# Output weights of a linear-attention block in four products by head group, re-blocked through DRAM, and phi(K) in one vector step

## The chip, the cores and the metric

The kernel runs on one core of one Trainium2 chip. The core has a matrix engine (TensorE, PE), a vector engine (DVE), a scalar engine (ACT), a general engine (GpSimd, POOL) and a queue engine (SyncE, SP) that issues most of the DMAs. Weight loads of TensorE are listed apart as PEld. Each engine works through its own queue in order and waits on semaphores. The metric is the device time of one execution in microseconds (us); the time before is 190.59 us, the median of three runs (190.52 to 190.61).

## The reference

The input x has 2048 tokens of 448 numbers, in bf16. The first half is a linear-attention block with 16 heads of 28, the second half a gated feed-forward block of width 1792. Cut to what matters:

```python
def phi(t): return where(t > 0, t + 1, exp(t)) + 1e-6
q, k, v = heads(layernorm(x) @ wqkv)
kv  = einsum("bhsd,bhse->bhde", phi(k), v)      # per head, summed over all tokens
z   = einsum("bhsd->bhd", phi(k))
num = einsum("bhqd,bhde->bhqe", phi(q), kv)
den = einsum("bhqd,bhd->bhq", phi(q), z) + 1e-6
h   = x + (num / den) @ wo
y   = layernorm(h)
out = h + (gelu(y @ w_gate) * (y @ w_up)) @ w_down
```

## The kernel before

**Tiles.** The tokens are sixteen tiles of 128 rows (t = 0 to 15), and from the query stage on eight pairs of tiles (p = 0 to 7). Channels of the attention come as four groups of four heads, 112 channels each.

**Stage 1, layer norm and projections.** Each tile of x is normalised (statistics at lines 413 and 414), transposed (tiles 0 to 3 on TensorE at line 443, the others by DMA at line 455) and projected to K and Q (line 469). The normalised tile xnn is padded with a column block of ones, so it is 512 wide. For K, ACT takes the exponential (`ek`, line 480), DVE clamps it (`ck`, line 481) and DVE forms phi(K) = max(k, eps) + clamped exponential (`pk`, line 482). Four products per tile (line 488) add xnn-transposed times phi(K) into four PSUM banks over all tiles. The ones give z in the last bank. Most Q projections are held back, as filler for the next stage.

**Stage 2, kv and the output weights.** The four banks are evicted (lines 514 to 521: `z1`, `z0`, `evpD_3`, `evpA_0`, `evpA_1`, `evpD_2`). Sixteen small products with the value weights (line 527, `kv`) give kv for each head. DVE masks it into `kvz` (line 531, `kvm`), laid out with zeros between the groups and a copied piece (`kvd`, line 536). Seven products (line 547) multiply it by wo, so that the result `w2` stands in four row blocks of 128, 128, 128 and 64 channels; the first three blocks get contributions from two head groups each, hence seven. Two DMAs (`dws0`, `dws1`) copy the halves of three blocks crosswise into `w2s`, so that each 64-row block exists in both halves of the partitions.

**Stage 3, query pairs.** For a pair p, DVE and POOL make phi(Q) and the denominators (`cqP`, `aqP`, `t1p`, `drP`, `rdP`, lines 582 to 589) and the normalised query (`pnP`, line 590). It is transposed, for pair 0 on TensorE (line 599) and for the others by a DMA that SP issues (`oT_p`, line 605). The attention output is the transposed query times `w2`. Pair 0 uses eight full products (line 617, `out1_0` and `out1_1`). Pairs 1 to 7 use fourteen products of 64 rows in two passes (lines 627 and 628, `outA_p` and `outB_p`): two such products run at the same time in the two row halves of TensorE, one for each tile of the pair. The second pass waits for the first to end, since it swaps the halves.

**Stage 4, feed-forward.** DVE adds the residual (`hr_t`, line 633), takes statistics, and the normalised tile is transposed (`hT_t`, line 665). Gate and up are computed in chunks: `gu2_v` for two tiles (chunks 0 to 13) and `gu4_v` for four (14 to 55), lines 731 and 733, 64-row products in both halves. ACT applies gelu (line 751, `ge`), DVE multiplies (line 753, `hm`). Even chunks use PSUM banks 0 and 6, odd ones 1 and 7, so a chunk starts only when both `hm` of the chunk two before it are done. The down products are `downA_p`, `downB_p` (line 697) and line 678 at the end.

**What sets the order.** Every piece of work is a task with a number, in the sequence in which the code creates it. `ORDERS` lists, engine by engine, the numbers in the order of that engine's queue; the waits follow from which task reads or writes which buffer. `HOLD` says, for tasks with several waits, which one is put first. The order around the change on TensorE is: `q_5 q_4 kv q_7 q_8 w2_2 w2_0 w2_1 q_9 w2_3 tro_1 tro_0 q_6 out1_1 out1_0 q_10 ... q_14 q_15 trh_1 trh_0 outA_1 outB_1 gu2_0 gu2_1 outA_2 gu2_2 gu2_3 outB_2`. On SP it is: `dwg0 dwu0 dwg1 dwu1 dws0 dws1 oT_1 oT_2 dwd oT_3`, where `dwg`, `dwu` and `dwd` load the gate, up and down weights.

Of the kernel before, what the change touches and what calls it, by code (L numbers as in the profile page):

```python
# [822 lines left out]
```

## Time and profile before

| what | value |
|---|---|
| median of three runs | 190.59 us |
| span of the profiled execution, first to last instruction | 188.3 us |
| TensorE busy | 184.3 us, 98% |
| DVE busy | 129.3 us, 69% |
| ACT busy | 76.5 us, 41% |
| POOL busy | 50.0 us, 27% |
| granted TensorE clock | 1.000 |

The span leaves out what lies around the first and last instruction, 2.3 us against the median. Busy time of TensorE includes the time in which a product drains through the engine, which overlaps the next product. The pace of a stage is therefore read from the distance between the starts of two instructions. In the rows of the timeline the columns are start, length, engine, line, operation, output and inputs, shape and count; in brackets stands the idle time before and what ended it. In the rows of groups the columns after the count are busy us, mean ns of one, and the idle time before.

### The profile page before, as it was taken

Reading aid. Unit: us, or ns where it says so; the run is one execution under the profiler, and the core shown is the slowest. Engines: PE = TensorE matmul, PEld = TensorE weight load, DVE = VectorE, ACT = ScalarE, POOL = GpSimd, SP = SyncE. Lnnn points to the kernel's source line nnn. Section 1 sums busy time; section 2 is a strip of 40 time slices with the busy share of each in tenths; the row PEclk is TensorE's granted clock in tenths of the full one; section 3 lists DMA queues with packets and bytes.
Section 4 is the critical chain, followed back from the end, with each engine's and each line's share of the span. In section 5 each row is a group of like instructions: output and inputs, shape, how many; then the busy total and the mean of one; then the engine's idle time right before and its main releaser. Section 6 shows DMA issues by size and latency. Waiting matters only on the chain.

```text
span 188.3 us, 4459 instructions
## 1 busy us (share of the span) xinstructions
PE 184.3 (98%) x1813; PEld 109.2 (58%) x1813; DVE 129.3 (69%) x330; ACT 76.5 (41%) x220; POOL 50.0 (27%) x91
## 2 busy tenths in 40 slices
PE   7999999999999999999999999999999999999994
PEld 7545555555688788965554555555545545454554
DVE  4999959999899998786796762562645244335432
ACT  3878752799963231432234222321242222224100
POOL 6067910704505686033614000206100000000000
PEclk9999999999999999999999999999999999999999
DMA  5996458999393526820005720000096000002024
GB/s 169 387 231 88 96 104 194 218 222 174 65 320 64 95 52 116 84 52 0 0 3 98 144 54 0 0 3 2 3 135 111 3 0 24 3 0 98 3 79 140
DMA packets 35076, 17.11 MB, mean 91 GB/s; under 512 B 26864, under 2 KB 33648, under 8 KB 35056
## 3 DMA queue, kind: packets, MB, share of 16 engines
q1 hardware_dynamic: 34432, 16.32, 41.1%
q10 hardware_dynamic: 624, 0.52, 0.8%
q8 instruction: 14, 0.23, 0.5%
q14 instruction: 6, 0.05, 0.1%
HBM read 8.26 MB, written 1.84 MB: 54 GB/s over the span
## 4 chain that ended last, share of the span: by engine, by line
PE 94%; DVE 3%; DMA 1%; issue 0%
PE ps L733 38%; PE ps L697 19%; PE ps L469 12%; PE ps L731 9%; PE ps L488 6%; PE ps L627 3%; PE ps L678 3%; PE ps L628 2%; DMA x_sb<-in_A_x_dram 1%; DVE st L413 1%; PE ps L617 1%; PE ps L547 1%; PE ps L527 1%; PE ps L443 0%; PE ps L654 0%; DVE den L572 0%
## 5 line engine op out<-in xcount | busy, mean ns | idle before, releaser
L733 PE MATMUL ps<-hnT,wgu_sb 64*128 64x512 bf16 (+1 forms) x490 | 88.8, 333 | 0.0
L731 PE MATMUL ps<-hnT,wgu_sb 64*128 64x512 bf16 (+1 forms) x490 | 88.6, 333 | 0.0
L751 ACT ACTIVATE gl<-ps 128x256 bf16<-128x256 f32 x112 | 36.6, 383 | 85.3 <-PE ps L731 84.4
L753 DVE TENSOR_TENSOR hh<-ps,gl 128x256 bf16<-128x256 f32 x112 | 42.1, 416 | 41.4 <-ACT gl L751 41.3
L733 PEld LDWEIGHTS ps<-hnT,wgu_sb 64*128 64x128 bf16 x490 | 45.2, 94 | 32.9 <-DVE hh L753 3.4
L731 PEld LDWEIGHTS ps<-hnT,wgu_sb 64*128 64x128 bf16 x490 | 45.4, 94 | 2.5
L697 PE MATMUL ps<-wd_sb,hh 64*128 64x448 bf16 x392 | 41.5, 349 | 0.0
L697 PEld LDWEIGHTS ps<-wd_sb,hh 64*128 64x128 bf16 x392 | 23.2, 94 | 14.5
L469 PE MATMUL ps<-wqk_sb,xnT 128*128 128x448 bf16 x128 | 27.4, 353 | 0.0
L413 DVE BATCH_NORM_STATS2 st<-x_sb 128x6 f32<-128x448 bf16 x32 | 19.2, 612 | 1.8 <-DMA x_sb<-in_A_x_dram 1.7
L585 POOL TENSOR_TENSOR t<-pq,zbc 128x448 f32<-128x448 bf16 x12 | 12.3, 1042 | 23.7 <-DVE pq L583 22.0
L469 PEld LDWEIGHTS ps<-wqk_sb,xnT 128*128 128x128 bf16 x128 | 11.9, 98 | 11.4 <-DVE pk L482 0.8
L488 PE MATMUL ps<-pk,xnn 128*128 128x448 bf16 x64 | 13.9, 352 | 0.0
L627 PE MATMUL ps<-w,pqnT 64*128 64x448 bf16 x49 | 11.5, 349 | 0.1
L425 POOL TENSOR_SCALAR ln<-mv 128x2 f32<-128x2 f32 x7 | 2.0, 291 | 35.2 <-DVE mv L414 35.0
L480 ACT ACTIVATE e<-ps 128x448 bf16<-128x448 f32 x16 | 8.5, 539 | 5.6 <-PE ps L469 5.5
L628 PE MATMUL ps<-pt_sb,pqnT 64*128 64x448 bf16 x42 | 10.2, 350 | 0.0
L633 DVE TENSOR_TENSOR x_sb<-ps,x_sb 128x448 bf16<-128x448 f32 x16 | 9.6, 616 | 0.7 <-PE ps L628 0.6
L662 POOL TENSOR_SCALAR hn<-x_sb,nm,rs 128x448 bf16<-128x448 bf16 x14 | 9.9, 719 | 0.4
L482 DVE SCALAR_TENSOR_TENSOR pk<-ps,e 128x448 bf16<-128x448 f32 x16 | 9.8, 617 | 0.1
L488 PEld LDWEIGHTS ps<-pk,xnn 128*128 128x128 bf16 x64 | 6.3, 98 | 5.9 <-DVE pk L482 0.3
L453 POOL TENSOR_SCALAR xnn<-x_sb,nm,rs 128x448 bf16<-128x448 bf16 x12 | 8.9, 744 | 2.2 <-ACT rs L422 1.9
(85 smaller groups left out, 160.5 us busy)
## 6 DMA issues: line engine op xcount, KB each, us to landing
out_dram<-x_sb SPq DMA_DIRECT2D x15, 112.0 KB, 1.8
wd_sb<-in_B_w_down_dram SPq DMA_DIRECT2D x1, 1568.0 KB, 8.4
x_sb<-in_A_x_dram SPq DMA_DIRECT2D x3, 448.0 KB, 5.9
wgu_sb<-in_B_w_gate_dram SPq DMA_DIRECT2D x1, 896.0 KB, 12.1
wgu_sb<-in_B_w_up_dram SPq DMA_DIRECT2D x1, 896.0 KB, 16.5
wgu_sb<-in_B_w_gate_dram SPq DMA_DIRECT2D x1, 672.0 KB, 6.1
wgu_sb<-in_B_w_up_dram SPq DMA_DIRECT2D x1, 672.0 KB, 8.5
wo_sb<-in_A_wo_dram SPq DMA_DIRECT2D x1, 392.0 KB, 7.5
```

The lines of the kernel that those rows point to most:

```text
L413: op("dve", lambda e: e.bn_stats(st[:, t, :], src_ap), [b_src], [b_st[t]], "bnst%s_%d" % (tag, t))
L469: ins = e.matmul(ps[:, bk, 0:D], xnT[:, t, k, :], wqk_sb[:, k, c0:c0 + D], start=(k == 0), stop=(k == 3))
L488: ins = e.matmul(ps[:, BK_PT[c], 0:D], xnn[:, t % XN_R, c * 128:(c + 1) * 128], pk[:, ip, :], start=(t == 0), stop=(t == T - 1))
L585: op("pool", lambda e, n=n: e.tensor_tensor(t1[:, n, :], pq[:, a + n, :], zbc[:, :], ALU.mult), [b_pq[a + n]] + b_z, [b_t1[n]], "t1p_%d" % ...
L627: e.matmul(ps[:, BK_OUT[0], 0:D], pqnT[ra, i2, sg // 2, :], w2[ra, sg // 2, :], start=(sg == 0), stop=(sg == 5))
L628: ins = e.matmul(ps[:, BK_OUT[1], 0:D], pqnT[rb, i2, 3 + (sg + 1) // 2, :], (w2 if sg == 6 else w2s)[rb, sg // 2, :], start=(sg == 0), sto ...
L662: op("pool", lambda e, t=t, sh=sh: e.tensor_scalar(hn[:, sh, 0:D], x_sb[:, t, :], nm2[:, t:t + 1], rs2[:, t:t + 1], ALU.add, ALU.mult), [b ...
L697: ins = e.matmul(ps[:, bko[half][n], 0:D], hh[rows, j, sl[n]], wd_sb[rows, j, :], start=(j == 0 and (half == 0 or p == 6)), stop=(j == NJ ...
L731: first = e.matmul(psG[:, jj * N:(jj + 1) * N], wgu_sb[A_, k, j * 128:(j + 1) * 128], hnT[A_, ka_, c0:c0 + N], start=(k == 0), stop=(k == ...
L733: ins = e.matmul(psU[:, jj * N:(jj + 1) * N], wgu_sb[B_, k, j * 128:(j + 1) * 128], hnT[B_, kb_, c0:c0 + N], start=(k == 0), stop=(k == NK ...
L751: G.add("act", lambda e, gi=gi, cs_=cs_, psG=psG: e.activation(gl[:, gi, cs_], psG[:, cs_], AF.Gelu_apprx_tanh), r=[b_ps[BK_G[i]]], w=[b_g ...
L753: op("dve", lambda e, dst=dst, srcU=srcU, srcL=srcL: e.tensor_tensor(dst, srcU, srcL, ALU.mult), [b_ps[BK_U[i]], b_glh], [b_ar[j_][t % HR] ...
```

## The change

The change has five parts.

1. *phi(K) in one step.* A row of ones is written into the padding of the K weights (`w1row`), where the normalised tile has ones, so the projection gives k + 1. ACT takes exp(k + 1 - 1) with a bias of -1. One DVE operation forms max(min(e, 1), k + 1). The clamp `ck` is gone. The 1e-6 of phi is added later: `pk` gets an extra column of 1e-6 (`pkeps`), the sums get a 449th column, and the evictions add it (`ecol` copies two such columns for ACT; z gets 2048 x 1e-6).
2. *Output weights by head group.* `kvz` holds the masked kv densely; four products of 112 rows each give `w2g`, one block for each head group. `kvd`, the zero padding of `kvz` and the two crosswise copies are gone.
3. *Pairs 0 and 1 use `w2g` as it is*, with eight products for a pair. Their normalised queries are written with each group padded to 128 columns, so the transposition of pair 1 has 1024 columns, not 896.
4. *Pairs 2 to 7 keep their 64-row products.* The blocks come through DRAM: one DMA writes `w2g` to a DRAM buffer (`dw2w`), two DMAs read it back as seven blocks of 64 rows into each half of the partitions (`dw2r0`, `dw2r1`). The buffer `w2p` lies over the sums and the value weights, which are dead by then.
5. *New orders and holds.* All five queues are ordered anew, and `HOLD` names one wait for most tasks. On TensorE the order around the change is now: `q_5 q_9 kv q_4 q_7 w2_1 w2_0 w2_2 q_8 w2_3 tro_0 tro_1 q_6 out1_0 out1_1 q_10 ... q_14 q_15 trh_0 trh_1 out1_2 out1_3 gu2_0 gu2_1 gu2_2 gu2_3 outA_2 gu2_4 outB_2 gu2_5 gu2_6 outA_3 downA_0 outB_3 gu2_7`. On SP: `dwg0 dwu0 dwg1 dwu1 oT_1 dw2w dw2r0 dw2r1 oT_2 dwd oT_3`. On DVE, after the output of pair 1: `hr_2 hr_3 bnst2_2 bnst2_3 drP_3 hm1_0 hm0_0 bnag2_3 bnag2_2 rdP_3 cqP_5 hm1_1 hm0_1 cqP_7 pnP_3 hm0_2 hm1_2 aqP_5 hm1_3 cqP_4 cqP_6 hm0_3 wrap_2 wrap_3 aqP_4 hr_5 hm0_4 hm1_4`. On ACT, `evhA_0` now comes before `eq_15`. On POOL, one memset of `pqn` and `mhalf` now come before `ones`, which the warm-up products read.

```diff
+        pv_sb = sb("pv_sb", [128, 8, D], BF16)
+        pt_sb, wv_sb, w2p = pv_sb[:, 0:4, :], pv_sb[:, 4:8, :], pv_sb[:, 0:NK, :]
...
-        pk = sb("pk", [128, PK_R, D], BF16)
+        pk = sb("pk", [128, PK_R, D + 2], BF16)
...
-        w2 = sb("w2", [128, 4, D], BF16)
+        w2g = sb("w2g", [GW, NG, D], BF16)
+        w2d = nc.dram_tensor("w2_bounce", [D, D], BF16)
...
+        op("dve", lambda e: e.memset(wqk_sb[64:65, 3, D:2 * D], 1.0), [b_wpad[0]], [b_w1r], "w1row")
...
-        op("pool", lambda e: e.memset(kvz[:, GW:15 * GW], 0.0), [], [b_kvm], "kvzpad")
+        for i_ in range(2):
+            op("pool", lambda e, i_=i_: e.memset(pqn[:, i_, :].rearrange("p (n g c) -> p n g c", n=2, g=NG)[:, :, :, GW:128], 0.0), [], b_pqn[i_], "pqnpad_%d" % i_)
...
-            eks.append(act_exp(lambda e: e.activation(e1[:, i, :], psK, AF.Exp), [b_ps[bk]], [b_e1[i]], "ek_%d" % t))
-            op("dve", lambda e: e.tensor_scalar(e1[:, i, :], e1[:, i, :], 1.0 + EPS, 0.0, ALU.min, ALU.max), [b_e1[i]], [b_e1[i]], "ck_%d" % t)
-            op("dve", lambda e: e.scalar_tensor_tensor(pk[:, ip, :], psK, EPS, e1[:, i, :], ALU.max, ALU.add), [b_ps[bk], b_e1[i]], [b_pk[ip]], "pk_%d" % t)
+            eks.append(act_exp(lambda e: e.activation(e1[:, i, :], psK, AF.Exp, bias=neg1[:, 0:1]), [b_ps[bk], b_neg1], [b_e1[i]], "ek_%d" % t))
+            op("dve", lambda e: e.scalar_tensor_tensor(pk[:, ip, 0:D], e1[:, i, :], 1.0, psK, ALU.min, ALU.max), [b_ps[bk], b_e1[i]], [b_pk[ip]], "pk_%d" % t)
...
-                        ins = e.matmul(ps[:, BK_PT[c], 0:D], xnn[:, t % XN_R, c * 128:(c + 1) * 128], pk[:, ip, :], start=(t == 0), stop=(t == T - 1))
+                        ins = e.matmul(ps[:, BK_PT[c], 0:D + 1], xnn[:, t % XN_R, c * 128:(c + 1) * 128], pk[:, ip, 0:D + 1], start=(t == 0), stop=(t == T - 1))
...
+        op("dve", lambda e: e.tensor_copy(ecol[:, 0:2], ps[:, BK_PT[0]:BK_PT[0] + 2, D]), [b_ps[BK_PT[0]], b_ps[BK_PT[1]]], [b_ecol], "ecol")
...
-                for g in gs:
-                    ins = e.matmul(ps[:, BK_W2[c], 0:D], kvc(g, c), wo_sb[:, g, :], start=(g == gs[0]), stop=(g == gs[-1]))
...
+        for g in range(NG):
+            G.add("pe", lambda e, g=g: e.matmul(ps[0:GW, BK_W2[g], 0:D], kvz[:, g * GW:(g + 1) * GW], wo_sb[:, g, :], start=True, stop=True),
+                  r=[b_kvm, b_wo], w=[b_ps[BK_W2[g]]], name="w2_%d" % g)
...
-        for h, (to, of) in enumerate(((A_, B_), (B_, A_))):
-            dma("sp", w2s[to, :, :], w2[of, 0:3, :], [b_w2s[h]], "dws%d" % h, r=b_w2[0:3], after=xts[-1:])
+        dma("sp", w2d.ap().rearrange("(g p) n -> p g n", p=GW), w2g[:, :, :], [b_w2d], "dw2w", r=b_w2, after=xts[-1:])
+        for h, rows in enumerate((A_, B_)):
+            dma("sp", w2p[rows, :, :], w2d.ap().rearrange("(k p) n -> p k n", p=64), [b_w2p[h]], "dw2r%d" % h, r=[b_w2d])
...
-                G.add("sp", lambda e, i2=i2: e.dma_start_transpose(pqnT[:, i2, 0:NK, :], pqn[:, i2, 0:2 * D]),
+                G.add("sp", lambda e, i2=i2: e.dma_start_transpose(pqnT[:, i2, 0:8 if p == 1 else NK, :], pqn[:, i2, 0:1024 if p == 1 else 2 * D]),
...
-            if p == 0:
+            if p < 2:
...
-                            ins = e.matmul(ps[:, BK_OUT[n], 0:D], pqnT[:, i2, 4 * n + g, :], w2[:, g, :], start=(g == 0), stop=(g == NG - 1))
+                            ins = e.matmul(ps[:, BK_OUT[n], 0:D], pqnT[0:GW, i2, 4 * n + g, :], w2g[:, g, :], start=(g == 0), stop=(g == NG - 1))
...
-                            e.matmul(ps[:, BK_OUT[0], 0:D], pqnT[ra, i2, sg // 2, :], w2[ra, sg // 2, :], start=(sg == 0), stop=(sg == 5))
-                            ins = e.matmul(ps[:, BK_OUT[1], 0:D], pqnT[rb, i2, 3 + (sg + 1) // 2, :], (w2 if sg == 6 else w2s)[rb, sg // 2, :], start=(sg == 0), stop=(sg == 5))
+                            e.matmul(ps[:, BK_OUT[0], 0:D], pqnT[ra, i2, sg // 2, :], w2p[ra, sg, :], start=(sg == 0), stop=(sg == 5))
+                            ins = e.matmul(ps[:, BK_OUT[1], 0:D], pqnT[rb, i2, 3 + (sg + 1) // 2, :], w2p[rb, sg, :], start=(sg == 0), stop=(sg == 5))
```

More of the change, by code (lines that the diff above doesn't have):

```diff
@@ L258, in bass_sequential_preLN__linear_attn_block__glu_gated_geglu__prompt_kernel @@
         wqk_sb = sb("wqk_sb", [128, 4, 2 * D], BF16)
-        wv_sb = sb("wv_sb", [128, 4, D], BF16)
+        pv_sb = sb("pv_sb", [128, 8, D], BF16)
+        pt_sb, wv_sb, w2p = pv_sb[:, 0:4, :], pv_sb[:, 4:8, :], pv_sb[:, 0:NK, :]
         wo_sb = sb("wo_sb", [GW, NG, D], BF16)
@@ L290, in bass_sequential_preLN__linear_attn_block__glu_gated_geglu__prompt_kernel @@
         eps_d = sb("eps_d", [128, 1], F32)
+        neg1 = sb("neg1", [128, 1], F32)
+        eps_s = sb("eps_s", [128, 1], F32)
+        ecol = sb("ecol", [128, 2], F32)
         rd = sb("rd", [128, 4, H], F32)
@@ L297, in bass_sequential_preLN__linear_attn_block__glu_gated_geglu__prompt_kernel @@
         gl = sb("gl", [128, 3, 512], BF16)
-        kvz = hh[0:GW, 6:9, :].rearrange("p a b -> p (a b)")
-        w2s = pt_sb[:, 0:3, :]
+        kvz = hh[0:GW, 6, 0:D]
         ps = es.enter_context(nc.psum_tensor("ps", [128, 8, 512], F32))
@@ L315, in bass_sequential_preLN__linear_attn_block__glu_gated_geglu__prompt_kernel @@
             _Buf(n) for n in ("ident", "ones", "mones", "mtmp", "mask", "eps", "mhalf", "powtmp"))
-        b_epsd = _Buf("epsd")
+        b_epsd, b_epss, b_ecol, b_neg1, b_pke, b_w1r = _Buf("epsd"), _Buf("epss"), _Buf("ecol"), _Buf("neg1"), _Buf("pke"), _Buf("w1r")
         b_st1, b_mv1, b_nm1, b_ln1, b_rs1 = bufs("st1", T), bufs("mv1", T), bufs("nm1", T), bufs("ln1", T), bufs("rs1", T)
@@ L383, in bass_sequential_preLN__linear_attn_block__glu_gated_geglu__prompt_kernel @@
         op("pool", lambda e: e.memset(eps_d[:], EPS), [], [b_epsd], "epsd")
+        op("pool", lambda e: e.memset(neg1[:], -1.0), [], [b_neg1], "neg1")
+        op("pool", lambda e: e.memset(eps_s[:], S * EPS), [], [b_epss], "epss")
+        op("pool", lambda e: e.memset(pk[:, :, D:D + 2], EPS), [], [b_pke], "pkeps")
         op("pool", lambda e: e.memset(mhalf[:], -0.5), [], [b_mhalf], "mhalf")
@@ L392, in bass_sequential_preLN__linear_attn_block__glu_gated_geglu__prompt_kernel @@
         op("pool", lambda e: e.memset(pt_sb[:, 3, :], 0.0), [], [b_pt[3]], "ptpad")
-        op("pool", lambda e: e.memset(pqn[:, 0, :].rearrange("p (n c) -> p n c", n=2)[:, :, D:512], 0.0), [], b_pqn[0], "pqnpad")
-        op("pool", lambda e: e.memset(kvz[:, GW:15 * GW], 0.0), [], [b_kvm], "kvzpad")
+        for i_ in range(2):
+            op("pool", lambda e, i_=i_: e.memset(pqn[:, i_, :].rearrange("p (n g c) -> p n g c", n=2, g=NG)[:, :, :, GW:128], 0.0), [], b_pqn[i_], "pqnpad_%d" % i_)
         tbl1 = G.add("act", lambda e: e.preload_act_table_set("natural_log_exp_and_others"), name="tbl1", kind="nosync", after=[tx1])
@@ L626, in foutp @@
                             ra, rb = (A_, B_) if sg % 2 == 0 else (B_, A_)
-                            e.matmul(ps[:, BK_OUT[0], 0:D], pqnT[ra, i2, sg // 2, :], w2[ra, sg // 2, :], start=(sg == 0), stop=(sg == 5))
-                            ins = e.matmul(ps[:, BK_OUT[1], 0:D], pqnT[rb, i2, 3 + (sg + 1) // 2, :], (w2 if sg == 6 else w2s)[rb, sg // 2, :], start=(sg == 0), stop=(sg == 5))
+                            e.matmul(ps[:, BK_OUT[0], 0:D], pqnT[ra, i2, sg // 2, :], w2p[ra, sg, :], start=(sg == 0), stop=(sg == 5))
+                            ins = e.matmul(ps[:, BK_OUT[1], 0:D], pqnT[rb, i2, 3 + (sg + 1) // 2, :], w2p[rb, sg, :], start=(sg == 0), stop=(sg == 5))
                         return ins
-                    parts.append(G.add("pe", foutp, r=b_pqnT[i2] + b_w2 + b_w2s, w=[b_ps[b_] for b_ in BK_OUT], name="out%s_%d" % (part, p), sync=parts[-1:]))
+                    parts.append(G.add("pe", foutp, r=b_pqnT[i2] + b_w2p, w=[b_ps[b_] for b_ in BK_OUT], name="out%s_%d" % (part, p), sync=parts[-1:]))
             for t in (a, a + 1):
```

47 lines of the change are left out of this document (16 added, 31 removed), and 143 rows, old and new, of tables (HOLD, ORDERS).

## The prediction

> **What bounds the kernel now.** I read the engine summary first, then the chain of waits, then TensorE's own timeline, and only then the queues that feed it. Here are the span and the busy shares, and what the chain is made of:
>
> ```profile
> span 188.3 us, 4459 instructions
> PE 184.3 (98%) x1813; PEld 109.2 (58%) x1813; DVE 129.3 (69%) x330; ACT 76.5 (41%) x220; POOL 50.0 (27%) x91
> ...
> PE 94%; DVE 3%; DMA 1%; issue 0%
> ```
>
> TensorE (PE) is nearly the whole chain, so an edit on another engine counts only where it stops PE. Busy is no proof of pace, because matmuls overlap; the pace is the distance from one start to the next. TensorE's timeline around the changed stages (start, us, then the piece):
>
> ```profile
> 34.23 1.68 PE L469 MATMUL ps<-wqk_sb,xnT 128*128 128x448 bf16 x8
> 35.96 1.03 PE L527 MATMUL ps<-pt_sb,wv_sb 128*112 128x112 bf16 x16
> ...
> 38.34 1.30 PE L547 MATMUL ps<-wo_sb,hh 112*128 112x448 bf16 x6
> 39.48 0.92 PE L469 MATMUL ps<-wqk_sb,xnT 128*128 128x448 bf16 x4
> 40.24 0.35 PE L547 MATMUL ps<-wo_sb,hh 112*128 112x448 bf16 x1
> ...
> 41.63 1.68 PE L617 MATMUL ps<-w,pqnT 128*128 128x448 bf16 x8
> 43.15 4.70 PE L469 MATMUL ps<-wqk_sb,xnT 128*128 128x448 bf16 x24
> ...
> 48.57 0.36 PE L627 MATMUL ps<-w,pqnT 64*128 64x448 bf16 x1
> ...
> 49.14 0.35 PE L627 MATMUL ps<-w,pqnT 64*128 64x448 bf16 x1
> ...
> 49.56 0.36 PE L627 MATMUL ps<-w,pqnT 64*128 64x448 bf16 x1
> ...
> 50.14 0.27 PE L733 MATMUL ps<-hnT,wgu_sb 64*128 64x256 bf16 x1
> ...
> 53.20 0.35 PE L628 MATMUL ps<-pt_sb,pqnT 64*128 64x448 bf16 x1
> ...
> 53.95 0.27 PE L733 MATMUL ps<-hnT,wgu_sb 64*128 64x256 bf16 x1
> ```
>
> Eight 448-column products take 41.63 to 43.15, so 0.19 us each, whether 112 rows high (L547, 38.34 to 39.48, six) or 128. Two 64-row products run together: one pair of them also takes 0.19. Two gate/up chunks of two tiles take 50.14 to 53.20, so 1.53 each. In this table PE stands still twice: 0.22 before kv (34.23 + 8 x 0.19 = 35.74, start 35.96) and 0.23 between the two passes of pair 1's output (49.14 + 0.19 = 49.33, start 49.56). After 50 us PE has no idle time in the waits of the profile. So PE work removed before 50 us pays in full, if VectorE (DVE) and the queues can follow.
>
> **The change part by part.**
>
> *Step 1, output weights.* Seven products (L547) become four: 3 x 0.19 = -0.57. They stand between query projections on PE's queue, so this is on the path. The copy `kvd` goes; the evictions stay four.
>
> *Step 2, pair 1's output.* 7 paired steps plus the stop last 48.57 to 50.14 = 1.57. Eight 112-row products with no second pass take 1.52: -0.05. Pair 0 keeps its eight.
>
> *Step 3, one extra column* in 64 products (L488): 64 x 0.19/448 = +0.03.
>
> *Step 4, phi(K) in one step.* DVE loses sixteen L481, 4.2 us:
>
> ```profile
> L481 DVE TENSOR_SCALAR e<-e 128x448 bf16<-128x448 bf16 x16 | 4.2, 271 | 2.3 <-ACT e L480 2.2
> L482 DVE SCALAR_TENSOR_TENSOR pk<-ps,e 128x448 bf16<-128x448 f32 x16 | 9.8, 617 | 0.1
> L536 DVE COPY hh<-hh 112x64 bf16<-112x64 bf16 x1 | 0.1, 140 | 0.0
> L531 DVE TENSOR_TENSOR hh<-ps,mask 112x448 bf16<-112x448 f32 x1 | 0.6, 614 | 0.0
> ```
>
> A window of the K stage (busy us of PE, PEld, DVE, ACT and POOL, then the granted clock and the DMA share):
>
> ```profile
> 15.00:20.00 5.00, 5.00 (x28) 2.53 (x27) 5.00 (x15) 4.69 (x15) 3.72 (x9) 1.00 0.61 89
> ```
>
> Both PE and DVE are full, and PE doesn't stop, so I count the 4.2 at 0. It buys slack that the new order spends by preparing later query pairs early. The exponential's bias and the bias row in the weights are free on instructions that exist; the row's memset comes before DVE has any x to work on. If `pk` at a 450-element pitch were slower, up to 16 x 0.05 would still be inside the slack of 4.2. The new POOL memsets (0.1 to 0.2 each) replace the larger `kvzpad`. Two of them now go before `ones`, so the warm-up matmuls start about 0.2 later; tile 0's transposes are held longer by DVE anyway: 0.
>
> *Step 5, evicting the K sums.* New: `ecol`, between 0.14 (L536) and 0.6 (L531, also from PSUM), after the last K sum and before ACT's two evictions; the other evictions become additions at the same 0.6. The old queue had one more op (`aq_1`) before its last eviction, and the new one has `ecol` and one reduction more, but starts earlier because the last `pk` is early. Kv's wait of 0.22 may go or double: -0.2 to +0.2, and I take -0.1, as every K tile now ends one op sooner.
>
> Sum at the first gate/up chunk: -0.57 - 0.05 + 0.03 - 0.1 = -0.7, so it could start at 49.45 instead of 50.14. Its bank 0 is read by `eq_15`, which ACT now runs behind the eviction of the first hnT block instead of ahead of it:
>
> ```profile
> 48.84 0.95 ACT L658 ACTIVATE hnT<-ps 128x896 bf16<-128x896 bf16 x1
> ```
>
> That is 0.95 later on ACT, nearly all of which the eight products of pair 1 cover: +0.1.
>
> *Step 6, the place of pair 2's output.* This is the dear part. DVE's queue after pair 1's output:
>
> ```profile
> 50.34 1.16 DVE L633 TENSOR_TENSOR x_sb<-ps,x_sb 128x448 bf16<-128x448 f32 x2 [0.58 <-PE ps L628]
> 51.42 0.62 DVE L413 BATCH_NORM_STATS2 st<-x_sb 128x6 f32<-128x448 bf16 x1
> 51.95 1.07 DVE L586 TENSOR_REDUCE den<-t 128x32 f32<-128x896 f32 x1
> 53.10 0.76 DVE L753 TENSOR_TENSOR hh<-ps,gl 128x256 bf16<-128x256 f32 x2
> ```
>
> The third chunk (gu2_2) needs the PSUM banks of the first, which are free when the two L753 have ended, at 53.10 + 0.76 = 53.86; PE starts it at 53.95. Before, pair 2's first pass (outA_2, 53.20 to 53.95) stood ahead of it and filled exactly that wait. After, its weights come back from DRAM later, and the order puts outA_2 behind gu2_3. DVE's new queue from the end of pair 1's output is hr_3, bnst2_2, bnst2_3, drP_3, hm1_0, hm0_0: 0.20 + 0.54 + 0.53 + 0.53 + 0.97 + 0.76 + 0.09 = 3.6 (starts above; 0.97 for the reduction, from the row below). PE has two chunks, 3.06, and 0.1 of Step 5's wait: it stands about +0.45.
>
> ```profile
> 45.16 1.05 DVE L586 TENSOR_REDUCE den<-t 128x32 f32<-128x896 f32 x1
> 46.13 0.69 DVE L645 TENSOR_SCALAR hn<-x_sb,mv,rs 128x448 bf16<-128x448 bf16 x2
> ```
>
> From there I added up DVE's new order in the same way, each group's mean less the 0.08 by which successive DVE ops overlap (L633: 0.62 long, 0.54 apart). Up to the product that frees gu2_6's bank DVE has twenty-one ops, 7.35, and 0.15 of waiting for pair 2's output, from 53.0 to 60.5; PE has four chunks and the two passes, 4 x 1.53 + 7 x 0.19 = 7.45, from 53.1 to 60.55. Gu2_6 is just in time, and gu2_3, gu2_4 and gu2_5 are 0.2 to 0.9 early: 0, with little to spare.
>
> *Step 7, the detour through DRAM.* Two SBUF copies go; one write and two reads come, on SP's queue behind oT_1 and ahead of oT_2 and the w_down load:
>
> ```profile
> 42.35 7.18 SPq L605 DMA_TRANSPOSE pqnT<-pqn  x2
> ...
> 48.30 1.23 SPq L605 DMA_TRANSPOSE pqnT<-pqn  x1
> ```
>
> and DMAs by issuing line (KB, then median us from issue to landing):
>
> ```profile
> out_dram<-x_sb SPq DMA_DIRECT2D x15, 112.0 KB, 1.8
> wd_sb<-in_B_w_down_dram SPq DMA_DIRECT2D x1, 1568.0 KB, 8.4
> ...
> wo_sb<-in_A_wo_dram SPq DMA_DIRECT2D x1, 392.0 KB, 7.5
> wqk_sb<-in_A_wqkv_dram ACTq DMA_DIRECT2D x1, 336.0 KB, 4.2
> ...
> pt_sb<-w SPq DMA_DIRECT2D x2, 168.0 KB, 5.7
> ...
> pqnT<-pqn SPq DMA_TRANSPOSE x7, 3.0
> ```
>
> oT_1 goes out near 42.3 as before (pn_3 keeps its place; eight blocks instead of seven are covered, as it has 5 us) and holds the queue 1.3. The 392 KB write leaves at 43.6 and lands after 1.8 to 5.7: 45.4 to 49.3. The two reads leave 0.6 apart behind it and land after 4.2 to 7.5: 50 to 57.5. SP waits for the write, and oT_2 is queued there: it goes at 48.3 as before, or up to 50.5, and lands 3.0 later. The w_down load follows by 1.3 and takes 8.4: 58 to 60.5. PE wants outA_2 at 49.5 + 3.06 + 0.45 + 3.06 = 56.1, and w_down some 6.8 later (two chunk pairs less one chunk, and the passes), near 62.9. I take 53 for the reads, as the weight loads that slowed the 5.7 and 7.5 rows are over by 46 us: cover 3 us, cost 0. With the upper end, PE would stand 1.4.
>
> The Trainium skill (DMA: Bandwidth & Descriptors, Anatomy of one DMA) gives a DMA about 2.0 us fixed plus its bytes at 436 GB/s; an estimate by it is 2.9 us for the write and 3.8 for both reads, so back by 51. By that rule the 168 KB copies would take 2.4, where the trace has 5.7 under load: the trace is the harder bound, and the sum is the same by both.
>
> **Sum.** -0.7 + 0.1 + 0.45 = -0.15, and nothing after 56 us, where the PE work is equal: span 188.1. The runs' median is 190.59, 2.3 above the profiled span; with the same 2.3: **190.4 us**. A difference under 0.2% (0.38 us) is about what a measurement of this kernel can't tell from no change.
>
> **The rivals.**
>
> *A, the stall of Step 6 is given back elsewhere (faster).* For it: PEld waits 12 times for L753 in the run before,
>
> ```profile
> PEld ps L733 <- DVE hh L753: 3.4, 12, 0.4
> ```
>
> and DVE arrives with 4.2 us less work. Then only the PE work counts, and 0.1 to 0.2 of those waits may be PE's own and go too: 190.59 - 0.6 - 0.2 = 189.8. Against it: hr_3 can't start before pair 1's output ends, so the 3.6 doesn't shrink with slack won earlier.
>
> *B, the copy through DRAM is late (slower).* The write's completion decides: if it lands after about 50, both reads, oT_2 and w_down are late together. At the upper ends PE stands 1.4 at outA_2 and less at the first down pass: 190.4 + 1.0 to 1.4 = 191.6. For it: 5.7 us for 168 KB in this very stretch. Against it: that copy met the gate/up loads, this one only their end.
>
> *C, DVE's new order misses at gu2_6 and at the K tiles (slower).* Margins under 0.1 at gu2_6 and at the PSUM slots of K6 and K8; 0.1 to 0.3 each at three or four places: 191.1.
>
> *D, the full pace comes late (slower).* The warm-up shows that there is such a change of pace:
>
> ```profile
> 1.05 4.43 PE L407 MATMUL ps<-ones_bf 128*128 128x128 bf16 x40 [1.05 <-POOL eps_d L383]
> 5.29 0.41 PE L443 MATMUL ps<-ident,xnn 128*128 128x128 bf16 x4
> ```
>
> Forty products of 128 columns from 1.05 to 5.29 are 0.106 each, 0.83 ns a column; later 448 columns take 0.19, 0.42 ns a column, though the granted clock reads 1.00 in the window above and in every other. So the full pace comes after about 4.2 us of work. A warm-up 0.2 later moves this by 0.2 at most, hidden; only if the pace rises at fixed instants, and one is missed, is some 2 us of work done at half pace, +1.2: 191.6. The Trainium skill (TensorE: Matmul & The Clock Gate, Part 1: The HAM clock gate) has such a free-running window of about 3.4 us; the 4.2 fits a start inside one, and no run here shows where the windows lie.
>
> **How the numbers follow.** Forecast 0.40 (190.0 to 190.9: mostly within 0.2%, 0.27; faster 0.08, slower 0.05); A 0.27; B 0.18; C 0.11; D 0.04. Faster 0.08 + 0.27 = 0.35, same 0.27, slower 0.05 + 0.33 = 0.38. The range reaches from just under A, 189.6, to B, 191.6; the forecast's own is 190.0 to 190.9.
>
> **What would show it.** Right: four L547-like products between the projections; pair 1's eight products in 1.5 us with no stop; first gate/up chunk near 49.5; a PE stop of 0.4 to 0.5 before the third chunk, released by DVE's product into hh; outA_2 without a wait; the down passes and all that follows 0.1 to 0.3 earlier than before. Wrong: no stop at the third chunk (A); PE or PEld waiting for a DMA at outA_2 or at the first down pass (B); several short waits on DVE before 35 us or at gu2_6 (C); K products at 0.38 us after 5.5 us (D).

## The result, and the profile after

The changed kernel takes 191.94 us in the median (191.53 to 192.23), 1.0067 of the time before (95% interval 1.0055 to 1.008): 1.3 us slower, just above the range given. The profiled execution has a span of 190.1 us, 1.8 more than before. By the spans recorded with each run, 188.3 belongs to an execution of about 190.3 us, so the profile of the kernel before is of one 0.3 faster than its median and that of the changed kernel of one 0.1 slower than its own: of the 1.8 below, the medians confirm 1.3.

First the summary of the changed kernel's page, and what its chain of waits is made of:

```profile
span 190.1 us, 4436 instructions
PE 185.0 (97%) x1804; PEld 108.8 (57%) x1804; DVE 127.6 (67%) x315; ACT 77.4 (41%) x220; POOL 50.5 (27%) x94
...
PE 78%; DVE 9%; DMA 8%; ACT 2%; issue 1%; SPq 0%
```

TensorE has nine instructions fewer, yet the span is longer, so TensorE stands still somewhere. Before, DMA was 1% of the chain; now it is 8%. TensorE's timeline shows where (rows answering those of the prediction, then the first passes of pairs 2 and 3, line 698):

```profile
18.79 0.92 PE L569 MATMUL ps<-pk,xnn 128*128 128x449 bf16 x4
20.01 1.29 PE L551 MATMUL ps<-wqk_sb,xnT 128*128 128x448 bf16 x6 [0.30 <-DMA xnT<-xnn]
...
36.96 1.00 PE L609 MATMUL ps<-pv_sb 128*112 128x112 bf16 x16
...
39.31 0.73 PE L618 MATMUL ps<-wo_sb,hh 112*112 112x448 bf16 x3
39.88 0.92 PE L551 MATMUL ps<-wqk_sb,xnT 128*128 128x448 bf16 x4
40.64 0.35 PE L618 MATMUL ps<-wo_sb,hh 112*112 112x448 bf16 x1
...
42.04 1.68 PE L688 MATMUL ps<-w2g,pqnT 112*128 112x448 bf16 x8
43.56 4.70 PE L551 MATMUL ps<-wqk_sb,xnT 128*128 128x448 bf16 x24
...
48.88 1.68 PE L688 MATMUL ps<-w2g,pqnT 112*128 112x448 bf16 x8
50.60 0.28 PE L802 MATMUL ps<-hnT,wgu_sb 64*128 64x256 bf16 x1
...
53.67 0.27 PE L802 MATMUL ps<-hnT,wgu_sb 64*128 64x256 bf16 x1
53.98 0.28 PE L804 MATMUL ps<-hnT,wgu_sb 64*128 64x256 bf16 x1
...
57.52 0.36 PE L698 MATMUL ps<-pv_sb,pqnT 64*128 64x448 bf16 x1 [0.30 <-DMA pqnT<-pqn]
...
63.85 0.36 PE L698 MATMUL ps<-pv_sb,pqnT 64*128 64x448 bf16 x1 [0.22 <-DMA pqnT<-pqn]
```

Kv (L609) starts at 36.96 instead of 35.96: 1.00 is lost before it. Pair 0's output ends 0.41 later (43.56 against 43.15), so the four products of the output weights won back 0.6. The first gate/up chunk starts 0.46 later (50.60 against 50.14). After that there are stops before the third chunk (53.67 to 53.98, its second bank), before outA_2 (57.52) and before outA_3 (63.85), the last two released by the transposes of the normalised queries. The waits of the changed kernel between 30 and 75 us name the releasers, TensorE's and its weight loads' (us in total, times, longest):

```profile
PEld ps L698 <- DMA pqnT<-pqn: 1.1, 2, 0.6
...
PE ps L698 <- DMA pqnT<-pqn: 0.5, 2, 0.3
PEld ps L802 <- ACT eq L577: 0.5, 1, 0.5
PEld ps L609 <- DVE pv_sb L603: 0.4, 1, 0.4
...
PEld ps L804 <- DVE hh L824: 0.3, 1, 0.3
```

The row with the bracket counts only a part of a stop, because the weight load ahead of the product waits too. A stop is therefore taken from starts: the start of a piece less the start of the piece before it and that piece's own length at full pace. Added up over the order of TensorE's queue, before against after:

| place | before | after | difference |
|---|---|---|---|
| first K product starts | 6.32 | 6.94 | +0.62 |
| K stage, stop at 20 us | 0 | 0.46 | +0.46 |
| extra column, 64 products | 0 | 0.03 | +0.03 |
| stops before kv | 0.30 | 0.19 | -0.11 |
| output weights | 1.33 | 0.76 | -0.57 |
| pair 1's output with its stop | 1.57 | 1.52 | -0.05 |
| stop before hT and the first chunk | 0.10 | 0.21 | +0.11 |
| stop before the third chunk | 0 | 0.22 | +0.22 |
| stop before outA_2 | 0 | 0.57 | +0.57 |
| stop before outA_3 | 0 | 0.41 | +0.41 |

The sum is 1.69. At the start of the eighth chunk and of the down products after it the two kernels stand 1.70 apart, and from there on they run alike but for 0.1. So the time went to two places: the first 20 us, and the transposes of pairs 2 and 3. Two rows need care. The third chunk's 0.22 is counted on the row half of TensorE that had a free bank for one product; the half that waited stands 0.31, and 0.47 before outA_2. And the first row is one execution: with the changed order of the start, the first K product starts at 6.45 in `transpose_first` below and at 6.78 in `write_first` and `no_holds`, and with the old order, in eight kernels, at 6.29 to 6.47. So 0.62 is the upper end of what that order costs.

The queue of SP in the changed kernel (timeline; the second column is how long the issue held the queue):

```profile
43.17 2.24 SPq L676 DMA_TRANSPOSE pqnT<-pqn  x1
45.46 0.58 SPq L424 DMA_DIRECT2D w_bounce<-w2g  x1
49.07 1.26 SPq L424 DMA_DIRECT2D pv_sb<-w_bounce  x2
50.38 1.65 SPq L676 DMA_TRANSPOSE pqnT<-pqn  x1
52.07 0.59 SPq L424 DMA_DIRECT2D wd_sb<-in_B_w_down_dram  x1
56.55 2.25 SPq L676 DMA_TRANSPOSE pqnT<-pqn  x1
```

and its DMAs by issuing line (KB each, median us from issue to landing):

```profile
wd_sb<-in_B_w_down_dram SPq DMA_DIRECT2D x1, 1568.0 KB, 9.6
...
pv_sb<-w_bounce SPq DMA_DIRECT2D x2, 392.0 KB, 5.6
...
w_bounce<-w2g SPq DMA_DIRECT2D x1, 392.0 KB, 3.6
...
pqnT<-pqn SPq DMA_TRANSPOSE x7, 4.0
```

The median of the transposes went only from 3.0 to 4.0. The two that matter are far from it. Issue by issue, from the trace (issued, landed, and the difference):

| DMA | before | after |
|---|---|---|
| write of w2g | - | 45.46 to 49.05: 3.6 |
| first read | - | 49.07 to 53.31: 4.2 |
| second read | - | 49.70 to 56.62: 6.9 |
| oT_2 | 48.30 to 51.26: 3.0 | 50.38 to 57.47: 7.1 |
| w_down load | 49.57 to 57.93: 8.4 | 52.07 to 61.71: 9.6 |
| oT_3 | 56.28 to 59.18: 2.9 | 56.55 to 63.80: 7.3 |

oT_2 lands at 57.47 and the product that needs it starts at 57.52. It was issued behind the two reads and lands after them. oT_3 was issued behind the w_down load and lands after it, at 63.80; the product starts at 63.85.

The packets in the trace show whose bytes moved when. The 896 packets of the two reads (896 bytes each) go from 50.45 to 54.59, the 896 packets of oT_2 (256 bytes each) from 53.67 to 56.78, and the first packet of the w_down load goes at 56.74. So oT_2 has its first packet 3.3 after its issue, against 1.2 in the kernel before, and the load issued behind it moves next to nothing until it is through. In the same way the w_down load moves from 56.74 to 61.10 and the first packet of oT_3 goes at 61.07. One part of the 7.1 is not explained: between 55 and 56 us the DMA engines moved only 32 GB/s.

The start, DVE's queue in the changed kernel and then what TensorE does there:

```profile
3.28 1.15 DVE L495 BATCH_NORM_STATS2 st<-x_sb 128x6 f32<-128x448 bf16 x2 [1.08 <-DMA x_sb<-in_A_x_dram]
4.35 0.30 DVE L496 BATCH_NORM_AGGREGATE mv<-st 128x2 f32<-128x6 f32 x2
5.00 0.63 DVE L495 BATCH_NORM_STATS2 st<-x_sb 128x6 f32<-128x448 bf16 x1 [0.35 <-DMA x_sb<-in_A_x_dram]
5.54 0.38 DVE L517 TENSOR_SCALAR xnn<-x_sb,mv,rs 128x448 bf16<-128x448 bf16 x1
```

```profile
5.98 0.79 PE L525 MATMUL ps<-ident,xnn 128*128 128x128 bf16 x8 [0.31 <-DVE xnn L517]
6.94 0.92 PE L551 MATMUL ps<-wqk_sb,xnT 128*128 128x448 bf16 x4 [0.17 <-ACT rs L504]
```

and the same two steps in the kernel before:

```profile
4.83 0.36 DVE L435 TENSOR_SCALAR xnn<-x_sb,mv,rs 128x448 bf16<-128x448 bf16 x1
...
6.32 1.11 PE L469 MATMUL ps<-wqk_sb,xnT 128*128 128x448 bf16 x4
```

The new order puts the statistics of tile 2 ahead of the normalisation of tile 0. Tile 2 is not there yet (its load lands at 4.98), DVE waits 0.35 for it, and the normalisation starts at 5.54 instead of 4.83.

### The profile page after: what moved, and what is told of

It reads as the page before. It is cut to its first block, busy times and chain, and to the rows that moved or that the text cites. A ratio compares the mean times of both kernels' runs of the same rounds, so it can differ in the third digit from the quotient of the medians.

```text
span 190.1 us, 4436 instructions
## 1 busy us (share of the span) xinstructions
PE 185.0 (97%) x1804; PEld 108.8 (57%) x1804; DVE 127.6 (67%) x315; ACT 77.4 (41%) x220; POOL 50.5 (27%) x94
## 4 chain that ended last, share of the span: by engine, by line
PE 78%; DVE 9%; DMA 8%; ACT 2%; issue 1%; SPq 0%
PE ps L804 34%; PE ps L768 19%; PE ps L551 7%; PE ps L802 6%; PE ps L569 4%; DMA pqnT<-pqn 4%; PE ps L749 3%; DVE st L495 3%; DMA xnT<-xnn 2%; DMA x_sb<-in_A_x_dram 2%; PE ps L698 2%; PE ps L699 1%; DVE x_sb L704 1%; DVE pk L563 1%; PE ps L688 1%
## 5 line engine op out<-in xcount | busy, mean ns | idle before, releaser
L768 PEld LDWEIGHTS ps<-wd_sb,hh 64*128 64x128 bf16 x392 | 23.8, 94 | 13.8
L551 PE MATMUL ps<-wqk_sb,xnT 128*128 128x448 bf16 x128 | 26.9, 353 | 0.5 <-DMA xnT<-xnn 0.3
L569 PE MATMUL ps<-pk,xnn 128*128 128x449 bf16 x64 | 13.7, 353 | 0.0
L563 DVE SCALAR_TENSOR_TENSOR pk<-e,ps 128x448 bf16<-128x448 bf16 x16 | 9.7, 614 | 4.8 <-ACT e L562 4.7
L704 DVE TENSOR_TENSOR x_sb<-ps,x_sb 128x448 bf16<-128x448 f32 x16 | 9.9, 617 | 3.5 <-PE ps L699 3.3
L562 ACT ACTIVATE e<-ps,neg 128x448 bf16<-128x448 f32 x16 | 9.9, 632 | 5.3 <-PE ps L551 5.3
L733 POOL TENSOR_SCALAR hn<-x_sb,nm,rs 128x448 bf16<-128x448 bf16 x14 | 11.3, 810 | 1.3 <-DMA hnT<-hn 1.0
L778 DVE TENSOR_TENSOR x_sb<-ps,x_sb 128x448 bf16<-128x448 f32 x12 | 7.4, 620 | 4.4 <-PE ps L768 4.4
L698 PE MATMUL ps<-pv_sb,pqnT 64*128 64x448 bf16 x42 | 9.9, 350 | 0.5 <-DMA pqnT<-pqn 0.5
L699 PE MATMUL ps<-pv_sb,pqnT 64*128 64x448 bf16 x42 | 9.9, 350 | 0.0
```

The source lines that it names most:

```text
L551: ins = e.matmul(ps[:, bk, 0:D], xnT[:, t, k, :], wqk_sb[:, k, c0:c0 + D], start=(k == 0), stop=(k == 3))
L569: ins = e.matmul(ps[:, BK_PT[c], 0:D + 1], xnn[:, t % XN_R, c * 128:(c + 1) * 128], pk[:, ip, 0:D + 1], start=(t == 0), stop=(t == T - 1))
L698: e.matmul(ps[:, BK_OUT[0], 0:D], pqnT[ra, i2, sg // 2, :], w2p[ra, sg, :], start=(sg == 0), stop=(sg == 5))
L699: ins = e.matmul(ps[:, BK_OUT[1], 0:D], pqnT[rb, i2, 3 + (sg + 1) // 2, :], w2p[rb, sg, :], start=(sg == 0), stop=(sg == 5))
L704: op("dve", lambda e, t=t, bo=bo: e.tensor_tensor(x_sb[:, t, :], ps[:, bo, 0:D], x_sb[:, t, :], ALU.add), [b_ps[bo], b_x[t]], [b_x[t]], "h ...
L768: ins = e.matmul(ps[:, bko[half][n], 0:D], hh[rows, j, sl[n]], wd_sb[rows, j, :], start=(j == 0 and (half == 0 or p == 6)), stop=(j == NJ ...
```

## The experiments

Two theories. **Theory Q**: the parts of the change are worth what they save, and the queues' new orders lose it, in two places (the start, and the DMAs of SP behind one another). **Theory P**: the parts themselves cost: phi(K) in one step, or the detour through DRAM wherever it stands. In the diffs below a queue is written by the names of its tasks; each experiment starts from the changed kernel where nothing else is said, and its times are medians with the ratio to the kernel before.

**The start in the old order** (`old_start`). DVE, TensorE and ACT up to tile 5 as before the change.

```diff
 DVE:
-bnst1_0 bnst1_1 bnag1_0 ... bnst1_2 normD_0 ... pk_0 bnst1_4 ...
+bnst1_0 bnag1_0 bnst1_1 bnag1_1 normD_0 bnst1_2 normD_1 bnag1_2 bnst1_3 ... bnst1_4 bnag1_4 bnst1_5 pk_0 ...
```

> The changed kernel with the start of the queues (TensorE, ACT and DVE up to the third K tile) in the order of the kernel before; nothing else. Theory Q (the new queue orders cost the time, not the parts themselves): the first K products start near 6.3 us instead of 6.94, the third K tile near 9.2 instead of 9.66, and as the DMA transposes of x then leave near 10.3 instead of 11.4, the wait of 0.46 us before the fifth K product group at 19 us goes too: span 0.6 to 0.9 us shorter, 189.2 to 189.5. Theory P (the new form of phi(K) and of the output weights costs the time): the longer exponential with a bias column (0.63 against 0.54 us) holds the start, and the span shortens by less than 0.3.

Measured: 191.11 us, 1.0024 (1.001 to 1.0038), 0.8 less than the changed kernel. The first K product starts at 6.47, the stop in the K stage is 0.13, and SP's queue is earlier by as much: oT_2 is issued at 49.72 and lands at 56.64 (6.9), oT_3 at 62.83, and the stops before outA_2 and outA_3 are 0.17 and 0.27. So the order of the start costs, and the two places are not independent.

**The write first** (`write_first`). One exchange on SP.

```diff
 SP:
-oT_1 dw2w dw2r0 dw2r1 oT_2 dwd oT_3
+dw2w oT_1 dw2r0 dw2r1 oT_2 dwd oT_3
```

> The changed kernel with the DRAM write of the output weights put ahead of the transposition of pair 1 in SP's queue; nothing else. Theory Q: the write leaves near 42 us instead of 45.5 and is done before pair 2's query is ready, so pair 2's transposition leaves near 49 instead of 50.4, and the stop of 0.57 us before pair 2's output is gone; the stop of 0.41 before pair 3's output, which I put down to the w_down load, stays: span 0.5 to 0.7 us shorter. Rival (the transposes are slow because of the traffic of the copy itself, wherever the write stands): the stop stays above 0.4.

Measured: 191.08 us, 1.0017 (1.0007 to 1.0027), 0.86 less. Its queue:

```profile
41.62 0.34 SPq L424 DMA_DIRECT2D w_bounce<-w2g  x1
42.79 2.10 SPq L676 DMA_TRANSPOSE pqnT<-pqn  x1
46.93 1.26 SPq L424 DMA_DIRECT2D pv_sb<-w_bounce  x2
48.64 1.25 SPq L676 DMA_TRANSPOSE pqnT<-pqn  x1
49.94 0.58 SPq L424 DMA_DIRECT2D wd_sb<-in_B_w_down_dram  x1
56.17 1.22 SPq L676 DMA_TRANSPOSE pqnT<-pqn  x1
```

The write takes longer (41.62 to 46.91, 5.3), but it leaves 3.8 earlier, so the reads leave 2.1 earlier and land at 51.1 and 53.0. oT_2 then takes 5.1 (48.64 to 53.73) and oT_3 4.0 (56.17 to 60.15). Both stops, 0.57 and 0.41, are gone. They belonged to the place of the write. The expectation had kept the second; it went because the w_down load leaves 2.1 earlier too and lands at 59.32 instead of 61.71, with oT_3 behind it.

**Both** (`both_orders`): the two edits above together.

> The changed kernel with the start in the old order and the DRAM write ahead of pair 1's transposition, both at once. Theory Q: the two gains are at different places of TensorE's queue (before 20 us, and at 55 to 64 us), but part of the second is already in the first run, whose stops at pairs 2 and 3 were 0.17 and 0.27 instead of 0.57 and 0.41: 190.2 to 190.5, at or under the time of the kernel before. Rival: they share one cause, and the time stays at 190.9 to 191.1.

Measured: 190.67 us, 1.0003 (0.9994 to 1.0012): not to be told from the kernel before. Together the two bring 1.27, not the 1.69 (0.83 and 0.86) of the two runs added, because each alone shortens the same waits for transposes. Against `write_first` the old start brings 0.41, with intervals that overlap and equal spans (188.8), so its own share is the less certain of the two. Left are the stops at the first chunk (0.21), the third (0.22) and about 0.5 in the K stage. They eat what the four products save.

**phi(K) alone** (`phik_alone`): the kernel before with the ones row, the biased exponential, the one-step `pk`, the 449th column and the new evictions, and the orders of before.

```diff
-ek_t ck_t pk_t   (exp; clamp; max and add)
+ek_t pk_t        (exp with bias -1; min and max), ecol ahead of the evictions
```

> The kernel before with phi(K) in one step and the late 1e-6 alone; the queue orders are those of before without the clamp, the column copy stands ahead of the first reduction on DVE. Theory Q: the same as before within 0.3 us (190.3 to 190.9). Theory P: slower by 0.4 to 0.9 us (191.0 to 191.5).

Measured: 190.64 us, 1.0007 (0.9992 to 1.0022). TensorE around kv:

```profile
34.35 1.68 PE L473 MATMUL ps<-wqk_sb,xnT 128*128 128x448 bf16 x8
36.26 1.00 PE L531 MATMUL ps<-pt_sb,wv_sb 128*112 128x112 bf16 x16 [0.23 <-DVE pt_sb L525]
```

Kv waits 0.39 for the eviction (34.35 + 8 x 0.19 = 35.87, start 36.26) instead of 0.22. Sixteen DVE operations less do not make the kernel faster, and the part does not make it slower. Theory P falls for phi(K).

**The output weights alone** (`w2_alone`): the kernel before with the four products, pair 1's full output and the detour through DRAM, with the write ahead of oT_1 and outA_2 behind gu2_2; phi(K) and the other orders as before.

> The kernel before with the output weights by head group, their use by pairs 0 and 1 and the trip through DRAM alone; phi(K) in two steps and the old orders, with the write ahead of pair 1's transposition and pair 2's first pass one gate/up chunk later. Theory Q: TensorE has 0.38 us less work and the stop of 0.24 us inside pair 1's output is gone: 189.9 to 190.2. Theory P: the trip through DRAM costs what it saves or more: 190.5 or above.

Measured: 191.31 us, 1.0046 (1.0028 to 1.0065). TensorE stops at two new places, here in its timeline:

```profile
41.14 0.62 PE L585 MATMUL ps<-ident,pqn 128*128 128x128 bf16 x8 [0.29 <-ACT w2g L536]
...
54.64 0.28 PE L719 MATMUL ps<-hnT,wgu_sb 64*128 64x256 bf16 x1 [0.50 <-DVE hh L739]
```

The transposes of pair 0 follow the last output weights so closely that they wait for ACT's eviction of them (0.46 by the starts), and the third chunk waits about 0.7 for DVE's two products into hh. DVE in turn waits for ACT:

```profile
53.83 0.76 DVE L739 TENSOR_TENSOR hh<-ps,gl 128x256 bf16<-128x256 f32 x2 [0.64 <-ACT gl L737]
```

ACT loads its table for gelu (ACT_TABLE_LOAD, 1.28 us from 51.84) and only then runs the gelu of the first chunk, 53.14 to 53.80. The kernel before has the same load (from 51.12) and the same wait, but outA_2 stands in it. A further 0.59 at a transpose of x falls in the K stage, which this edit does not touch. The time lies in the range of theory P, not in that of Q (189.9 to 190.2). The cause that P names does not show as a wait, as outA_2 starts without a stop; what the detour costs here is the place of outA_2. The part needs new orders around it; with the old ones it loses more than it saves.

**The transpose ahead of the reads** (`transpose_first`).

```diff
 SP:
-oT_1 dw2w dw2r0 dw2r1 oT_2 dwd
+oT_1 dw2w oT_2 dw2r0 dw2r1 dwd
```

> The changed kernel with pair 2's transposition put ahead of the two reads from DRAM in SP's queue; the write stays where it is. If a transposition is slow because of the loads issued ahead of it: it lands 3 to 4 us after its issue instead of 7.1, the reads leave 1.3 us later and land near 57, so that the stop before pair 2's output is 0.2 or less; pair 3's, behind the w_down load, stays: 0.4 to 0.6 us faster than the changed kernel. If it is slow because of the w_down load behind it: still 6 us or more, and the stop stays.

Measured: 191.59 us, 1.0057 (1.0044 to 1.007), not to be told from the changed kernel; the expected gain of 0.4 to 0.6 did not come. The row of outA_2 and its releaser:

```profile
57.35 0.35 PE L698 MATMUL ps<-pv_sb,pqnT 64*128 64x448 bf16 x1 [0.53 <-DMA pv_sb<-w_bounce]
```

oT_2, now ahead of the reads, goes from 48.63 to 51.58: 2.95, as in the kernel before. Here the reads and the w_down load both leave behind it; by the packets above, it was the reads that it had to wait for. But the second read lands at 57.22, and the stop passes to it, 0.80. Reads and transpose are both needed by the same product; exchanging them only changes which comes last.

**The w_down load early** (`wd_early`): the kernel before, with `dwd` ahead of `oT_2` on SP.

```diff
 SP:
-oT_1 oT_2 dwd oT_3
+oT_1 dwd oT_2 oT_3
```

> The kernel before with one place changed in SP's queue: the w_down load goes ahead of pair 2's transposition instead of behind it. If a transposition that is issued during a load's flight has to wait for the bytes queued ahead of it: it lands 5 us or more after its issue instead of 2.96, near 53.5 to 55, and TensorE stops 0.3 to 2 us at pair 2's first pass (53.2); pair 3's transposition keeps its 3 us. If the 7.1 us of the changed kernel came from the reads back from DRAM alone: 3 to 3.5 us as before, and no stop.

Measured: 190.86 us, 1.0013 (0.9996 to 1.003). The load goes out at 43.99 and lands at 52.12; oT_2, issued at 48.64, lands at 52.98. It takes 4.3 instead of 3.0, between the two expectations, and lands 0.86 after the load, with no detour in the kernel. TensorE wants outA_2 0.6 later than that, so no stop shows.

**No holds** (`no_holds`): the table of preferred waits emptied.

```diff
-HOLD = { ... }
+HOLD = {}
```

> The changed kernel with an empty HOLD, so that of several waits the one with the highest count is put first; nothing else. Both theories: no difference, within 0.1 us. Rival: the order of waits adds some ten ns at each of many hand-overs, and the time moves by more than 0.4 us.

Measured: 191.68 us, 1.0056 (1.0036 to 1.0076), within the changed kernel's interval. The holds are not the cause.

**The statistics' order alone** (`stats_order`): only the first eight entries of DVE's layer norm as before.

```diff
 DVE:
-bnst1_0 bnst1_1 bnag1_0 bnag1_1 bnst1_2 normD_0 ...
+bnst1_0 bnag1_0 bnst1_1 bnag1_1 normD_0 bnst1_2 normD_1 bnag1_2
```

> The changed kernel with only the first statistics on DVE in the old order (tile 0's aggregation and normalisation ahead of tiles 1 and 2). Theory Q, first half: the first K product starts near 6.4 instead of 6.9 and the time falls by 0.3 to 0.5 us; the wait for the transposes of x near 19 us stays, since they follow tile 4's statistics, which still stand behind the first phi(K). Rival: the start doesn't matter, since the transposes of x set the pace of the K stage; then less than 0.15 us.

Measured: 191.6 us, 1.0045 (1.0031 to 1.0058), 0.3 less than the changed kernel with overlapping intervals. The normalisation is early again, but the first K product is not:

```profile
5.29 0.40 PE L525 MATMUL ps<-ident,xnn 128*128 128x128 bf16 x4 [0.37 <-DVE xnn L517]
6.13 0.40 PE L525 MATMUL ps<-ident,xnn 128*128 128x128 bf16 x4 [0.43 <-DVE xnn L517]
6.90 0.92 PE L551 MATMUL ps<-wqk_sb,xnT 128*128 128x448 bf16 x4 [0.38 <-ACT rs L504]
```

Now ACT's order holds it (rs L504). The start is lost by two queues, and mending one of them shows the other.

**Two tries for more**, both from `both_orders`. `all_orders` has the ones for the warm-up first on POOL, `eq_15` ahead of ACT's eviction of hnT, and the statistics of tile 3 behind the first two `hm` on DVE. `best` has the first two of these, and outA_2 behind gu2_1.

```diff
 POOL: -pqnpad_1 ... ones      ACT: -evhA_0 ... eq_15     DVE (all_orders): -bnst2_3 drP_3 hm1_0 hm0_0
       +ones pqnpad_1               +eq_15 evhA_0                           +drP_3 hm1_0 hm0_0 bnst2_3
 PE (best): -gu2_0 gu2_1 gu2_2 gu2_3 outA_2
            +gu2_0 gu2_1 outA_2 gu2_2 gu2_3
```

> As both orders, and three more places put back: the memset that the warm-up waits for is first on POOL, the exponential that frees the first gate/up bank is ahead of the first hnT eviction on ACT, and the statistics of tile 3 stand behind the two products that free the third chunk's banks on DVE. Theory Q: the stops of 0.21 us each before the first and in the third gate/up chunk go, and about 0.15 at the start: 189.8 to 190.2, faster than before by 0.2 to 0.4%. Rival (the small stops are made up for elsewhere, or DVE is the limit there in any order): no different from both orders within 0.15.

> As both orders, with the memset that the warm-up waits for first on POOL, the exponential that frees the first gate/up bank ahead of the first hnT eviction on ACT, and pair 2's first pass one place earlier than in the old order's neighbour: behind the second gate/up chunk, where the kernel before has it. Theory Q: pair 2's query lands near 53.0, about when the second chunk ends, so the pass starts with a stop of 0.3 at most and then covers the 0.22 us by which the third chunk waited for DVE; with 0.2 to 0.3 at the start and at the first chunk the span is 188.2 to 188.5 and the time 190.0 to 190.3, 0.1 to 0.3% faster than before. Rival: pair 2's query is late by more than 0.5 us there, and the time is at or above both orders.

Measured: 190.99 us, 1.002 (1.001 to 1.003), and 191.22 us, 1.0031 (1.0021 to 1.0041). Neither beats `both_orders`, and both miss the expected 189.8 to 190.3. In `all_orders` the first chunk starts earlier (the stop of 0.21 becomes 0.10), but the stops before the third and fourth chunks are 0.31 and 0.43. DVE comes to the first chunk's products sooner and finds them not ready; from its waits there:

```profile
DVE hh L824 <- ACT gl L822: 0.4, 1, 0.4
```

ACT's table load (1.28 from 50.84) and the gelu behind it set the third chunk now, and the statistics moved behind the first two `hm` hold up the next two, for which the fourth chunk waits.

In `best` outA_2 fills the wait at the third chunk, as in the kernel before, and meets oT_2, which lands at 53.78 behind the reads:

```profile
53.82 0.36 PE L698 MATMUL ps<-pv_sb,pqnT 64*128 64x448 bf16 x1 [0.33 <-DMA pqnT<-pqn]
```

By the starts that stop is 0.49. A further 0.40 comes at gu2_6 (61.78), for DVE's product into hh, and 0.59 at a transpose of x in the K stage. So in this order the detour takes away the place that hid the wait at the third chunk. No version here beats the kernel before. Theory Q holds for phi(K) and for the two places of the loss; that the output weights are worth what they save, with the detour behind them, is not shown by any version.

## Why the prediction was wrong

The forecast was 190.4; the runs gave 191.94. By its steps:

*Step 1 (-0.57), Step 2 (-0.05), Step 3 (+0.03): right.* From the start of kv to the end of pair 0's output the changed kernel wins 0.59; pair 1's eight products take 1.52 without a second pass; TensorE's own work falls by 0.35, which is -0.57, +0.03 and +0.19 for pair 1, whose stop of 0.24 goes.

*Step 4 (0): right for phi(K), wrong for the start.* `phik_alone` shows the 0. The step called the exponential's bias free; it is not (below), but `phik_alone` is no slower for it. What failed is the sentence that costs the start at nothing because tile 0's transposes are held by DVE anyway. It looked only at the memsets on POOL. It did not follow DVE's and ACT's new orders of the first tiles, where normalisation comes behind statistics whose tile has not landed: 0.62 at the first K product in the profile. `old_start` gives 0.83 of the time back, part of it because SP's queue runs earlier, and `both_orders` 0.41 against `write_first`. The stop of 0.46 in the K stage belongs to it only in part: kernels with the same order of the start have 0.1 (`write_first`) to 0.72 (`no_holds`) there, by the arrival of a transpose of x, and what sets it is open.

*Step 5 (-0.1, and +0.1 at the first chunk): right*, -0.11 before kv and 0.21 at the first chunk by `eq_15`, while an old stop of 0.10 ahead of hT is gone.

*Step 6 (+0.45): right in kind and too large.* DVE's queue came out as summed, and the third chunk is released by DVE's product into hh; it takes 3.53 from the end of pair 1's output (48.88 + 1.52 = 50.40) to the end of that product (53.93), against 3.6. But the first chunk itself stood 0.21 instead of 0.1, and what TensorE waits there it needn't wait here: 0.31 is left on the half that waited, 0.22 as the table counts it. The step counted DVE's queue alone; ACT's gelu of the first chunk, behind its table load, ends at 53.39 in this trace, when DVE has just begun its products (53.18), so a shorter DVE queue would have won little; `all_orders` shows it. No stop came at gu2_6, as forecast; one of rival C's kind (0.40) appears in `best`.

*Step 7 (0): the main failure, with 0.98.* The write and the time of the wait were right: it landed at 49.05, between 45.4 and 49.3. The term that failed is "lands 3.0 later" for oT_2. 3.0 is the median of seven transposes, most of them with nothing large ahead of them that had still to land; this one is issued 1.3 behind two reads of 392 KB and takes 7.1, and oT_3 behind the w_down load takes 7.3. The kernel before had a sign of it: oT_1, issued behind the two crosswise copies, took 5.05 (42.35 to 47.40) and landed 0.86 after the second of them. Even the upper end given for its issue, 50.5, with 3.0 made 53.5, early enough. The reads were bounded to 57.5 and taken at 53; the second came at 56.62, 2.0 after its last packet, and what held it is open. `transpose_first` (2.95 ahead of the reads) and `wd_early` (4.3 behind a load alone) show that it is the place in the queue. The w_down load, issued 1.7 behind, is not the cause: its first packet goes when oT_2 is nearly through, and the kernel before has it 1.3 behind oT_2, which takes 3.0. `write_first` shows that an earlier write removes both stops.

*Rival B* had the right mechanism, DRAM copy, oT_2 and w_down late together, and 1.4 at its upper end. Its condition was too strict: the write need not land after 50. The down passes were not late. That its 191.6 lies near the 191.94 is partly luck, since only 0.98 of the losses came this way; 1.08 came at the start and at a transpose of x, which no rival named. A did not come, as the stop at the third chunk is there. D did not come either: the first four K products take 6.94 to 7.70, 0.19 each.

The Trainium skill (DMA: Bandwidth & Descriptors, Anatomy of one DMA), whose fit that section gives for one DMA issued from GpSimd, made an estimate of 2.9 us for the write and 3.8 for both reads, here issued from SP. Measured are 3.6, and 4.2 and 6.9 for the two reads; where the write meets the gate and up loads (`write_first`), 5.3. The same page (Issuing engines are not separate DMA queues) says that DMAs run on the same 16 engines and interleave with each other, whichever engine started them. The DMAs in question here all come from SP, so the trace shows a part of it only: packets of oT_2 and of the reads mix from 53.67 to 54.59, and otherwise the bytes go in the order of issue.

## What to carry to other kernels

Price a DMA at its place in the queue, not at its group's median: ask which bytes are issued ahead of it on its queue and not yet landed, and take the landing of these as the earliest time for it. In all thirteen traces, each transpose of the queries that left SP behind a DMA still in flight landed after that DMA, by 0.7 to 2.3 us. When all queues are ordered anew, walk every one of them from the first instruction, also in stages that the change does not touch; a saved product is worth 0.19 us, a normalisation behind the wrong load cost up to 0.6. And a piece of work that filled a wait (outA_2 before the third chunk) has a value of its own, which a later arrival of its data takes away.
